# One q load per pair of heads, k copies split between ScalarE and the DMA queue, cluster rows stored in one transfer

## The chip, the core and the metric

The kernel runs on one core of a Trainium2 chip. A core has five engines with an instruction queue each: TensorE (PE, matmuls into PSUM), VectorE (DVE), ScalarE (ACT), GpSimd (POOL) and SyncE (SP), which here only issues transfers; 16 DMA engines move the data. The metric is device time in microseconds, from one execution of the whole program; the median of several runs is compared. On this kernel a difference of about 0.5% is what the measurement can tell from none.

## The reference

Queries, keys and values have shape (2, 8, 768, 64): two batches, eight heads, 768 positions, head size 64. Each head has 16 centroids. Every query and every key is assigned to the centroid of largest cosine; a query sees only the keys of its own cluster. Two MLPs follow, each 512 to 2048 to 512 on 1536 tokens.

```python
q_assign = np.argmax(np.einsum('bhsd,hcd->bhsc', q_n, c_n), axis=-1)
k_assign = np.argmax(np.einsum('bhsd,hcd->bhsc', k_n, c_n), axis=-1)
mask = q_assign[:, :, :, None] == k_assign[:, :, None, :]
scores = scale * np.matmul(q, k.transpose(0, 1, 3, 2))
scores = np.where(mask, scores, -1000000000.0)
attn = softmax(scores)                      # exp, row sum, division
x = np.matmul(attn, v)                      # to (1536, 512)
h = x @ w_in;  x = (h * np.clip(h + 3, 0, 6) / 6) @ w_out
h = x @ w_in2; out = softplus(h) @ w_out2
```

## The kernel before

**Blocks and stages.** The tokens form six blocks of 256 (batch b, block u of three). For each block and head the attention makes two chunks of 128 queries by 768 keys (`chunk`): score matmuls on TensorE, the row maximum on VectorE (line 944), the exponential on ScalarE (line 952), the reciprocal of the sum. For the later blocks the attention weights are split into two float16 parts (`split`, lines 463 and 471: ScalarE makes the high part, VectorE the low part) and turned by a transposing DMA from `hl` into `pt` (line 985); earlier ones are turned by TensorE matmuls (line 977). `attend` multiplies with v (line 1053). The first MLP of a finished block is laid between the attention of later blocks (lines 654 to 656, 1116, 1136); the weights are decoded by VectorE (lines 529 to 531, 601 to 603). The second MLP fills the time from about 470 us on.

**Cluster rows.** `assign` makes for each pair of heads a tile `oh` of 128 partitions by 384: row 64t + 32n + 16*odd + c is cluster c of the query (t = 0) or key (t = 1) of one head, for half n of the sequence. `store` writes it to a scratch tensor `ohd` in HBM (line 806), as two transfers of 64 partitions; the destination of each is viewed as (half n, row c, position s). The rows come back as the lower 16 rows of the operands of the score matmul, which so adds the mask: `rows0` (lines 866 to 875) for the first block, line 889 into `qa` and line 918 into `ka` for the others. For the first pair `rows0` reads `oh` itself, without the scratch tensor.

**q and k of the later blocks.** `pair` loads q of two heads into a tile `qd` of 128 partitions, twice: once in the lower and once in the upper 64 partitions (line 885), both heads beside each other. `prep`, two heads ahead of its use, makes from it `qa` (64 rows of rounded q, then the cluster rows) and `qb` (in one half of the partitions the rounded q, in the other the remainder): two ScalarE instructions (lines 919, 920) and one of VectorE (line 921). From k it builds once per batch and head `kb`, rounded k and remainder (lines 914, 915). `ka` holds a copy of the rounded k, moved there by a DMA from `kb` (line 917), and the cluster rows. `ka` has two buffers, so the next but one head waits for the score matmuls of the one two before; `qb` has three, the pair's `qa` two, `qd` one.

**What sets the order.** The program is written out in a plan of steps with due times in units of a block (the table `K`: `a0` and `a1` for `assign`, `i` and `o` for the weights, `m` for the MLP, and so on). Then `own_order` lists all instructions, and `list_schedule` places each with a price from `estimate` at the earliest time that its inputs, its engine and its buffers allow; the order that comes out on each engine's queue, SP's among them, is fixed in the program. A transfer is priced there by an issue of 580 ns, a rate per kind (`RATE`), a fixed latency and one queue that all transfers share; `slack` is added between an instruction and its users on another engine. The engines keep to that order whatever the real times are.

Of the kernel before, what the change touches and what calls it, by code (L numbers as in the profile page):

```python
# [8 lines left out]
F32 = mybir.dt.float32  # L9
F32R = mybir.dt.float32r  # L10
# [3 lines left out]
ACTF = mybir.ActivationFunctionType  # L14
# [7 lines left out]
W1E = ['dve', 'dve']  # L22

K = {
    'slack': (800, 250),
    'asx': 3,
    'qx': -1,
    'f1': [0],
# [1 line left out]
    'look': {'PE': 0, 'Activation': 0},  # L30
    'pcp': 1,
    'r0p': [1, 2, 3, 4],
    'a0': [-1.153, -0.043, 0.103, 0.303],
    'v0': 0.133,
    'v1': 3.116,
    'a1': [2.095, 2.095, 2.993, 3.179],
    'i': [0.472, 0.641, 0.98, 1.067],
    'il': [0.357, 0.4, 0.334, 0.212],
    'o': [1.18, 1.511, 1.585, 1.882],
    'ol': [0.179, 0.246, 0.223, 0.145],  # L40
    'wd': 0.089,
    'm': [1.41, 2.61, 3.59, 4.703, 6.29],
    'ml': [0.976, 0.75, 1.125, 0.983, 1.339],
    'gq': 3,
    'gr': 1,
    'ahead': 2,
    'lag0': 0.008,
    'lag': 0.226,
    'pl': {},
    'ohb': 2,  # L50
    'gv': 2,
    'gk': [3, 0],
    'gi': [-1, -1, -1],
    'lead': 0,
    'w2o': [1.36, 1.527],
    'ly': [1.133],
    'p4': [-0.643, 0.833],
    'p5': [0.797, 0.627],
    'o1': [1.323, 0.41],
    'w2': [0, -0.047, -0.049, 0.272],  # L60
    's2': [9, 15],
    'ly2': [0],
    'mo': [2, 0, 3, 1],
    'P': '',
    'qs': '',
    'x0': [2, 2, 2],
    'f0': [0, 1],
    'ze': [0],
    'w2e': [4.497],
    'w2l': 0.213,  # L70
    'tg': (),
    'we': [(1,), (0,), (0,), (0,)],
    'sb': (2, 2),
    'w2d': 0.223,
    't3': 3.93,
    'w2s': 'left',
    'te': [1, 0, 1, 0, 0, 0, 0, 0, 1, 0, 1, 0, 0, 0, 0, 0],
    'dgb': 2,
    'v2': -0.878,
    'dge': 0,  # L80
    'pg': 1,
    'pk': 1,
    'dsp': [0, 1],
    'ro': 0,
    'vp': [0.262, 0.043, -0.149, -0.211],
    'eqp': [1, 1, 1, 0],
    'qdb': 1,
    'kbe': [1, 1, 1, 1],
    'dl': 300,
    'pl_': 100,  # L90
    'w2oe': ['dve', 'dve'],
}
# [17 lines left out]
}  # L110
POOLS = sorted(set(OVER) | {p for l in OVER.values() for p in l}, key=len, reverse=True)
WINDOW = 3413.3
RATE = {"raw<in_moe_w_in": 271, "raw<in_moe_w_out": 302, "raw<in_moe2_w_in": 239, "raw<in_moe2_w_out": 345, "ka<kb": 173, "qd<in_q": 118, "rk<in_k": 220, "st<in_v": 224, "ydram<ys": 243, "yl<ydram": 164, "ka<ohd": 276, "q0<in_q": 203, "k0<in_k": 201, "rq<in_q": 232, "ohd<oh": 265, "qa<ohd": 165, "k0<ohd": 99, "q0<ohd": 109, "k0<oh": 39, "q0<oh": 39, "cw<in_centroids": 63}


def elements(a):
# [6 lines left out]
def estimate(op, eng, ins, outs, inst, psum):  # L123


    n = max([elements(a) for a in ins + outs] or [0])
# [5 lines left out]
    if eng == "PE":  # L132
        cols, f32 = elements(ins[0]), str(ins[0].dtype)
        m = inst.tile_size[1]
        if f32 == "dt.float32":
            t = max(cols * m / 76.8, 1.75 * m) + (90 if cols > 256 else 45 if cols > 128 else 5 if m == 128 else 40 if m == 64 else 27)
        else:
            t = cols / 2.4 + (15 if "32r" in f32 else 2.5)
# [28 lines left out]
        return t - 40, t + 60, op in ("TensorScalarPtr", "TensorTensor", "TensorCopy")  # L167
    size = max(elements(a) * list(a.ap)[0][1] * SIZE.get(str(a.dtype), 4) for a in ins + outs)
    if op == "DmaTransposeAnt":
        return 1640, (size / 250, K['dl'] - 500), False  # L170
    rate = RATE.get(outs[0].bass_ap.tensor.name.rsplit("_", 1)[0] + "<" + ins[0].bass_ap.tensor.name.rsplit("_", 1)[0], 200)
    return 580, (size / rate, K['dl']), False


class Graph:
# [90 lines left out]
def list_schedule(g, slack):  # L266
# [49 lines left out]
    for _ in range(N):  # L316
# [33 lines left out]
        queues[e].append(k)  # L350
        free[e] = s + hold
        if isinstance(done, tuple):
            time, lat = done
            queue = max(s + hold + 500, queue) + time
            done = queue + lat
        else:
            if shared:
                port[e] = s + done - (30 if e == "DVE" else 60)
            done += s
# [38 lines left out]
def kernel(ctx: ExitStack, tc: tile.TileContext, qT, kT, v, cen, w1i, w1o, w2i, w2o, out):  # L398
# [24 lines left out]
    one_s = const.tile([128, 128], F32)  # L423
    nc.vector.memset(one_s, 1.0)

    ohd = dram.tile([B, NP, 2, 2 * C, S], F32)
    ydram = dram.tile([NB, 128, KD, TB], F32)

    def after(tile_, src):
# [5 lines left out]
    def pace(tile_):  # L435

        if 0 in paced:
            if K["pcp"]:
                after(tile_, paced[0])
            else:  # L440
                nc.vector.tensor_copy(out=tile_[:, 0:1].bitcast(F32), in_=paced[0])
# [424 lines left out]
    def rows0(h):  # L866

        p, odd = divmod(h, 2)
        for t, dst in ((1, K0[h][64:64 + C]), (0, Q0[p][64:64 + C, odd])):
            if p == 0:  # L870
                for n in range(2):
                    r0 = 64 * t + 32 * n + C * odd
                    nc.sync.dma_start(out=dst[:, n * SH:(n + 1) * SH], in_=oh[0, p][r0:r0 + C, :])
            else:
                nc.sync.dma_start(out=dst, in_=ohd[0, p, t, C * odd:C * odd + C])

    def pair(b, u, p):

        qs = slice(u * TB, (u + 1) * TB)
        qd = rqp.tile([128, 2, TB], F32, tag="qd", name="qd", bufs=K["qdb"])  # L880
        if b == 0 and u == 1 and 2 * p < K["gq"]:
            pace(qd[:, 0])
        src = qT[b, 2 * p:2 * p + 2, :, qs].rearrange("o d s -> d o s")
        for half in range(2):
            nc.sync.dma_start(out=qd[64 * half:64 * half + 64], in_=src)
        qa = kq.tile([64 + C, 2, TB], F32R, tag="qa", name="qa", bufs=2)
        dst = qa[64:64 + C].bitcast(F32)
        src = ohd[b, p, 0, :, qs].rearrange("(o c) s -> c o s", o=2)
        nc.sync.dma_start(out=dst, in_=src)
# [750 lines left out]
```

## Time and profile before

| | before |
|---|---|
| median of 3 runs | 770.31 us (767.09 to 770.63) |
| the profiled execution's own time | 774.19 us |
| its span, first to last instruction | 772.2 us |
| TensorE busy | 718.1 us (93%) |
| VectorE busy | 608.8 us (79%) |
| ScalarE busy | 515.7 us (67%) |
| GpSimd busy | 96.0 us (12%) |
| mean granted TensorE clock | 0.976 of full |
| moved by DMA | 103.03 MB, mean 133 GB/s |

The profiled execution's time holds the span and some 2 us around it. Busy shares are averages over stages of different kinds: attention with the first MLP to about 470 us, the second MLP after that. TensorE's matmuls are pipelined, so a busy TensorE need not be at its peak. The DMA share of a stretch is the mean busy share of the 16 DMA engines; as it is put together from packets' times, it can lie above 1 in short stretches. "Idle before" and "waits" name what ended the idle time of an engine.

### The profile page before, as it was taken

Reading aid. Unit: us, or ns where it says so; the run is one execution under the profiler, and the core shown is the slowest. Engines: PE = TensorE matmul, PEld = TensorE weight load, DVE = VectorE, ACT = ScalarE, POOL = GpSimd, SP = SyncE. Lnnn points to the kernel's source line nnn. Section 1 sums busy time; section 2 is a strip of 40 time slices with the busy share of each in tenths; the row PEclk is TensorE's granted clock in tenths of the full one; section 3 lists DMA queues with packets and bytes.
Section 4 is the critical chain, followed back from the end, with each engine's and each line's share of the span. In section 5 each row is a group of like instructions: output and inputs, shape, how many; then the busy total and the mean of one; then the engine's idle time right before and its main releaser. Section 6 shows DMA issues by size and latency. Waiting matters only on the chain.

```text
span 772.2 us, 15821 instructions
## 1 busy us (share of the span) xinstructions
PE 718.1 (93%) x6173; PEld 601.6 (78%) x6173; DVE 608.8 (79%) x1101; ACT 515.7 (67%) x897; POOL 96.0 (12%) x170
## 2 busy tenths in 40 slices
PE   5679779999989988899999989999999999999998
PEld 1355566788778867788888878897888888888887
DVE  3457698999968767797899986998999998925930
ACT  1338668787778876796777775666786368726931
POOL 6021532331220220001000300000000000000000
PEclk9989989999999999999999999999999999999999
DMA  8174554788999996989999997141441020010001
GB/s 185 38 216 146 159 180 148 190 198 199 222 194 193 201 167 138 158 171 203 210 198 204 206 215 190 57 164 52 141 136 43 29 69 2 1 42 16 1 15 41
DMA packets 170906, 103.03 MB, mean 133 GB/s; under 512 B 130064, under 2 KB 155408, under 8 KB 170832
## 3 DMA queue, kind: packets, MB, share of 16 engines
q1 hardware_dynamic: 170832, 102.04, 57.4%
q8 instruction: 48, 0.79, 0.4%
q14 instruction: 26, 0.21, 0.1%
HBM read 57.77 MB, written 7.86 MB: 85 GB/s over the span
## 4 chain that ended last, share of the span: by engine, by line
PE 72%; DMA 10%; DVE 10%; ACT 3%; issue 2%; POOL 2%; SPq 0%; ACTq 0%; DVEq 0%; POOLq 0%
PE s L941 7%; DMA pt<-hl 5%; PE h L1353 5%; PE h L1354 5%; PE h L1355 5%; PE y L655 5%; PE y L654 5%; PE y L656 5%; PE avt L1053 5%; PE h L654 4%; PE h L656 4%; PE h L655 4%; PE o L1518 3%; PE o L1519 3%; PE o L1520 3%
## 5 line engine op out<-in xcount | busy, mean ns | idle before, releaser
L944 DVE TENSOR_REDUCE nm<-s 128x1 f32<-128x768 f32 x96 | 90.8, 949 | 27.9 <-PE s L941 27.6
L654 PE MATMUL y<-g,w 128*128 128x256 f16 x384 | 105.9, 276 | 5.6 <-ACT ys L1136 4.9
L952 ACT ACTIVATE e<-s,nm 128x768 f32<-128x768 f32 x96 | 85.8, 894 | 37.5 <-DVE nm L948 17.3
L655 PE MATMUL y<-g,w 128*128 128x256 f16 x384 | 105.8, 275 | 1.4 <-DVE g L471 1.4
L656 PE MATMUL y<-g,w 128*128 128x256 f16 x384 | 105.8, 275 | 1.1 <-DVE w L471 1.1
L654 PE MATMUL h<-x,w 128*128 128x256 f16 x384 | 105.6, 275 | 0.0
L656 PE MATMUL h<-x,w 128*128 128x256 f16 x384 | 105.6, 275 | 0.0
L655 PE MATMUL h<-x,w 128*128 128x256 f16 x384 | 105.4, 275 | 0.0
L1354 PE MATMUL h<-y,w 128*128 128x256 f16 x336 | 90.8, 273 | 0.0
L1353 PE MATMUL h<-y,w 128*128 128x256 f16 x336 | 90.3, 273 | 0.0
L1355 PE MATMUL h<-y,w 128*128 128x256 f16 x336 | 89.7, 273 | 0.0
L655 PEld LDWEIGHTS <-w 128*128 128x128 f16 x768 | 75.9, 99 | 17.2 <-issue 8.4
L654 PEld LDWEIGHTS <-w 128*128 128x128 f16 x768 | 76.4, 100 | 15.8 <-issue 6.3
L656 PEld LDWEIGHTS <-w 128*128 128x128 f16 x768 | 76.1, 99 | 15.1 <-issue 4.6
L463 ACT ACTIVATE hl<-e,r 128x768 f16<-128x768 f32 x72 | 66.7, 929 | 28.7 <-DMA pt<-hl 21.7
L471 DVE SCALAR_TENSOR_TENSOR hl<-e,r,hl 128x768 f16<-128x768 f32 x72 | 73.3, 1025 | 14.9 <-ACT hl L463 14.1
L471 DVE SCALAR_TENSOR_TENSOR g<-a,sg,g 128x512 f16<-128x512 f32 x72 | 51.5, 744 | 4.2 <-ACT g L463 3.9
L941 PE MATMUL s<-kb,qb 128*128 128x384 f32 x160 | 49.2, 386 | 4.2 <-ACT e L952 4.1
L1053 PE MATMUL avt<-pt,v 128*64 128x256 f16 x648 | 46.9, 287 | 6.3 <-DMA pt<-hl 6.3
L977 PEld LDWEIGHTS tr<-dg,e 128*128 128x128 f32 x288 | 39.4, 209 | 14.3 <-issue 8.4
L463 ACT ACTIVATE g<-a,sg 128x512 f16<-128x512 f32 x72 | 48.5, 712 | 1.3 <-DVE a L1413 0.7
L1053 PEld LDWEIGHTS <-v 128*64 128x64 f16 x648 | 37.5, 115 | 14.8 <-issue 8.3
(234 smaller groups left out, 1685.9 us busy)
## 6 DMA issues: line engine op xcount, KB each, us to landing
raw<-in_moe_w_out_dram SPq DMA_DIRECT2D x32, 512.0 KB
raw<-in_moe_w_in_dram SPq DMA_DIRECT2D x8, 1024.0 KB
raw<-in_moe_w_in_dram SPq DMA_DIRECT2D x16, 512.0 KB
ka<-kb SPq DMA_DIRECT2D x40, 192.0 KB
qd<-in_q_dram SPq DMA_DIRECT2D x40, 128.0 KB
rk<-in_k_dram SPq DMA_DIRECT2D x12, 384.0 KB
st<-in_v_dram SPq DMA_DIRECT2D x12, 256.0 KB
ydram<-ys SPq DMA_DIRECT2D x12, 256.0 KB
```

What stands on the lines that cost most here:

```text
L463: nc.scalar.activation(out=hi, in_=src, func=ACTF.Copy, scale=scale)
L471: nc.vector.scalar_tensor_tensor(out=lo, in0=src, scalar=scale, in1=hi, op0=ALU.mult, op1=ALU.subtract)
L654: nc.tensor.matmul(out=ps, lhsT=wt.lhsT(kk, m, 0), rhs=xh, start=start, stop=False)
L655: nc.tensor.matmul(out=ps, lhsT=wt.lhsT(kk, m, 0), rhs=xl, start=False, stop=False)
L656: nc.tensor.matmul(out=ps, lhsT=wt.lhsT(kk, m, 1), rhs=xh, start=False, stop=stop)
L941: nc.tensor.matmul(out=s[:, n, 0:SH], lhsT=x[:, q], rhs=y[:, n * SH:(n + 1) * SH], start=i == 0, stop=i == len(pairs) - 1)
L944: nc.vector.tensor_reduce(out=nm, in_=sv, op=ALU.max, axis=AX.XY, negate=True)
L952: nc.scalar.activation(out=e.rearrange("p (a s) -> p a s", a=2), in_=sv, func=ACTF.Exp, bias=nm, scale=scale, accum_out=sm)
L1053: nc.tensor.matmul(out=a[64 * odd:64 * odd + 64, p % 2, :], lhsT=vt[:, kt, vi, odd, :], rhs=PT[2 * p + odd][:, pi * KT + kt, :], start=(kt ...
L1353: nc.tensor.matmul(out=ps[:, o, :], lhsT=hi, rhs=y[:, 0, kk], start=first and o == kk == 0, stop=False, skip_group_check=True)
L1354: nc.tensor.matmul(out=ps[:, o, :], lhsT=hi, rhs=y[:, 1, kk], start=False, stop=False, skip_group_check=True)
L1355: nc.tensor.matmul(out=ps[:, o, :], lhsT=lo, rhs=y[:, 0, kk], start=False, stop=kk == 1, skip_group_check=True)
```

## The change

Three things are done in another way, and the order is laid out anew.

1. `qd` holds each pair's q once, head 2p in the lower and head 2p + 1 in the upper 64 partitions: one transfer in place of two. `qa` and `qb` become two slots of one pair's tile of 128 partitions. One ScalarE instruction writes the rounded q into the lower 64 rows of both slots (64x512 by a repeated input), another one writes the 64 rows that VectorE subtracts from (64x256).
2. `ka`'s copy of the rounded k is made by ScalarE for odd heads (`kac` 0) and by the DMA for even heads (`kac` 3).
3. `ohd` keeps the halves of the sequence apart, in the order of `oh`'s partitions, so that `store` is one transfer of 128 partitions by 384. The loads of cluster rows are viewed accordingly; q's rows of the middle block (positions 256 to 511) cross the halves at 384 and are fetched in two transfers.
4. The table `K` has other due times and slack, and `estimate` prices transfers by one rate with a lead time in place of a rate per kind.

```diff
-    'slack': (800, 250),
+    'slack': (150, 300),
-    'a0': [-1.153, -0.043, 0.103, 0.303],
+    'a0': [-0.937, -0.118, 0.131, 0.512],
-    'a1': [2.095, 2.095, 2.993, 3.179],
+    'a1': [2.223, 2.078, 2.909, 3.267],
...
-    'dl': 300,
+    'dl': 200,
+    'kac': [3, 0],
...
-RATE = {"raw<in_moe_w_in": 271, "raw<in_moe_w_out": 302, ...}
+RATE = 272
...
     if op == "DmaTransposeAnt":
-        return 1640, (size / 250, K['dl'] - 500), False
-    rate = RATE.get(...)
-    return 580, (size / rate, K['dl']), False
+        return 1640, (size / 157, 400 + K["dl"], 800), False
+    return 580, (size / RATE, 850 + K["dl"], 1080), False
...
-            time, lat = done
-            queue = max(s + hold + 500, queue) + time
+            time, lat, lead = done
+            queue = max(s + lead, queue) + time
...
-    ohd = dram.tile([B, NP, 2, 2 * C, S], F32)
+    ohd = dram.tile([B, NP, 2, 2, 2 * C, SH], F32)
...
     def store(b, p):
-        for t in range(2):
-            nc.sync.dma_start(out=ohd[b, p, t].rearrange("c (n s) -> n c s", n=2), in_=oh[b, p][64 * t:64 * t + 64])
+        nc.sync.dma_start(out=ohd[b, p].rearrange("t n c s -> (t n c) s"), in_=oh[b, p])
...
-                nc.sync.dma_start(out=dst, in_=ohd[0, p, t, C * odd:C * odd + C])
+                nc.sync.dma_start(out=dst.rearrange("c (n s) -> c n s", n=2), in_=ohd[0, p, t, :, C * odd:C * odd + C].rearrange("n c s -> c n s"))
...
-        qd = rqp.tile([128, 2, TB], F32, tag="qd", name="qd", bufs=K["qdb"])
+        qd = rqp.tile([128, TB], F32, tag="qd", name="qd", bufs=K["qdb"])
...
-        src = qT[b, 2 * p:2 * p + 2, :, qs].rearrange("o d s -> d o s")
-        for half in range(2):
-            nc.sync.dma_start(out=qd[64 * half:64 * half + 64], in_=src)
-        qa = kq.tile([64 + C, 2, TB], F32R, tag="qa", name="qa", bufs=2)
-        dst = qa[64:64 + C].bitcast(F32)
-        src = ohd[b, p, 0, :, qs].rearrange("(o c) s -> c o s", o=2)
-        nc.sync.dma_start(out=dst, in_=src)
+        nc.sync.dma_start(out=qd, in_=qT[b, 2 * p:2 * p + 2, :, qs].rearrange("h d s -> (h d) s"))
+        qa = kq.tile([128, 2, 2, TB], F32R, tag="qa", name="qa", bufs=2)
+        dst = qa[64:64 + C, :, 1].bitcast(F32)
+        s0, s1 = qs.start, qs.stop
+        while s0 < s1:
+            n, e = s0 // SH, min(s1, (s0 // SH + 1) * SH)
+            src = ohd[b, p, 0, n, :, s0 - n * SH:e - n * SH].rearrange("(o c) s -> c o s", o=2)
+            nc.sync.dma_start(out=dst[:, :, s0 - u * TB:e - u * TB], in_=src)
+            s0 = e
...
-        qb = kq.tile([128, TB], F32R, tag="qb", name="qb")
...
-        nc.sync.dma_start(out=ka[0:64].bitcast(F32), in_=kb[here].bitcast(F32))
-        nc.sync.dma_start(out=ka[64:64 + C].bitcast(F32), in_=ohd[b, p, 1, C * odd:C * odd + C])
-        nc.scalar.activation(out=qb, in_=qd, func=ACTF.Copy, scale=0.125)
-        nc.scalar.activation(out=qa[0:64], in_=qd[0:64], func=ACTF.Copy, scale=0.125)
+        e = K["kac"][h % len(K["kac"])]
+        if e == 0:
+            nc.scalar.activation(out=ka[0:64], in_=kb[here].bitcast(F32), func=ACTF.Copy)
...
+        else:
+            nc.sync.dma_start(out=ka[0:64].bitcast(F32), in_=kb[here].bitcast(F32))
+        nc.sync.dma_start(out=ka[64:64 + C].bitcast(F32).rearrange("c (n s) -> c n s", n=2), in_=ohd[b, p, 1, :, C * odd:C * odd + C].rearrange("n c s -> c n s"))
+        qa, qb = qq[0:64 + C, 1], qq[:, 0]
+        if odd:
+            nc.scalar.activation(out=qb[here], in_=qd[here], func=ACTF.Copy, scale=0.125)
+            nc.scalar.activation(out=qq[0:64], in_=qd[here].unsqueeze(1).broadcast_to([64, 2, TB]), func=ACTF.Copy, scale=0.125)
+        else:
+            nc.scalar.activation(out=qq[0:64], in_=qd[here].unsqueeze(1).broadcast_to([64, 2, TB]), func=ACTF.Copy, scale=0.125)
+            nc.scalar.activation(out=qb[there], in_=qd[here], func=ACTF.Copy, scale=0.125)
         nc.vector.scalar_tensor_tensor(out=qb[here], in0=qd[here], scalar=0.125, in1=qb[here].bitcast(F32), op0=ALU.mult, op1=ALU.subtract)
```

The other entries of `K` that change are due times of the same kind (for v, the weights and the MLP steps).

## Rows read from the trace of the kernel before

**Rows 1.** Windows: us, busy us of each engine, clock, DMA share, GB/s

```profile
140.00:225.00 85.00, 79.87 (x685) 67.21 (x684) 78.87 (x160) 68.39 (x124) 21.58 (x35) 0.96 0.85 198
225.00:345.00 120.00, 111.61 (x1025) 94.85 (x1022) 91.73 (x164) 94.27 (x176) 17.89 (x34) 0.97 0.95 175
345.00:470.00 125.00, 122.25 (x1136) 104.11 (x1134) 108.07 (x193) 92.00 (x164) 11.77 (x22) 0.99 1.04 205
```

**Rows 2.** Waits of PE, in stretches 0:45, 45:100, 140:225 and 225:345

```profile
PE s L941 <- DMA k<-ohd: 7.0, 1, 7.0
PE s L941 <- DMA k<-ohd: 2.4, 1, 2.4
PE s L941 <- DMA ka<-ohd: 2.1, 1, 2.1
PE avt L1053 <- DMA pt<-hl: 3.9, 2, 2.5
PE y L654 <- ACT ys L1136: 3.7, 1, 3.7
```

**Rows 3.** Chain that ended last, whole span: start us, us, what

```profile
32.20 6.22 DMA ohd<-oh
73.42 6.71 DMA ohd<-oh
208.94 7.01 DMA ka<-ohd
266.76 9.24 DMA pt<-hl
276.87 0.83 ACT ys L1136 x2
298.23 6.47 DMA pt<-hl
399.18 8.25 DMA pt<-hl
```

**Rows 4.** Timeline of SP's issues, around three stores

```profile
31.65 1.03 SPq L806 DMA_DIRECT2D ohd<-oh  x2
36.60 0.31 SPq L875 DMA_DIRECT2D q<-ohd  x1
207.68 1.22 SPq L806 DMA_DIRECT2D ohd<-oh  x2
265.52 1.14 SPq L806 DMA_DIRECT2D ohd<-oh  x2
```

**Rows 5.** Windows of 1 and 4 us behind the stores

```profile
34.00:35.00 1.00, 0.00 (x0) 0.00 (x0) 0.83 (x2) 0.08 (x2) 0.00 (x0) 1.00 0.13 37
295.00:296.00 1.00, 1.00 (x11) 0.62 (x8) 1.00 (x2) 0.61 (x3) 0.60 (x1) 1.00 0.12 13
216.00:220.00 4.00, 3.91 (x17) 2.96 (x18) 2.89 (x6) 2.79 (x7) 0.00 (x0) 0.57 0.98 96
```

**Rows 6.** DMA issues by line, whole span

```profile
ka<-kb SPq DMA_DIRECT2D x40, 192.0 KB
qd<-in_q_dram SPq DMA_DIRECT2D x40, 128.0 KB
ohd<-oh SPq DMA_DIRECT2D x16, 96.0 KB
```

**Rows 7.** Groups by line, shapes apart: busy us, mean ns, idle before

```profile
L919 ACT ACTIVATE qb<-qd 128x256 fp32r<-128x256 f32 x40 | 16.0, 407 | 5.7 <-PE s L941 3.9 <-DMA qd<-in_q_dram 1.7
L920 ACT ACTIVATE qa<-qd 64x256 fp32r<-64x256 f32 x40 | 15.0, 406 | 4.5 <-DMA qd<-in_q_dram 3.5 <-POOL dg L966 0.8 <-PE s L941 0.2
L914 ACT ACTIVATE kb<-rk 64x768 fp32r<-64x768 f32 x16 | 13.4, 839 | 0.8 <-DMA rk<-in_k_dram 0.6
```

**Rows 8.** Waits of SP's queue, whole span

```profile
SPq L917 <- PE s L941: 19.2, 9, 9.1
SPq L917 <- ACT kb L914: 10.1, 3, 6.2
```

More of the change, by code (lines that the diff above doesn't have):

```diff
@@ L32 @@
     'r0p': [1, 2, 3, 4],
-    'a0': [-1.153, -0.043, 0.103, 0.303],
-    'v0': 0.133,
-    'v1': 3.116,
-    'a1': [2.095, 2.095, 2.993, 3.179],
[L37 to L43, printed above, removed]
+    'a0': [-0.937, -0.118, 0.131, 0.512],
+    'v0': 0.158,
+    'v1': 3.02,
+    'a1': [2.223, 2.078, 2.909, 3.267],
+    'i': [0.471, 0.639, 0.98, 1.067],
+    'il': [0.354, 0.399, 0.323, 0.205],
+    'o': [1.182, 1.511, 1.585, 1.881],
+    'ol': [0.179, 0.317, 0.272, 0.153],
+    'wd': 0.09,
+    'm': [1.41, 2.61, 3.59, 4.703, 6.383],
+    'ml': [0.98, 0.767, 1.125, 0.983, 1.25],
     'gq': 3,
@@ L46 @@
     'ahead': 2,
-    'lag0': 0.008,
-    'lag': 0.226,
+    'lag0': 0.029,
+    'lag': 0.23,
     'pl': {},
@@ L54 @@
     'lead': 0,
[L55 to L62, printed above, removed]
+    'w2o': [1.318, 1.319],
+    'ly': [1.067],
+    'p4': [0.105, 0.385],
+    'p5': [0.754, 0.522],
+    'o1': [1.695, 1.358],
+    'w2': [0, 0.292, -0.148, 0.768],
+    's2': [5, 12],
+    'ly2': [6],
     'mo': [2, 0, 3, 1],
@@ L68 @@
     'ze': [0],
-    'w2e': [4.497],
-    'w2l': 0.213,
+    'w2e': [4.39],
+    'w2l': 0.285,
     'tg': (),
@@ L73 @@
     'sb': (2, 2),
-    'w2d': 0.223,
-    't3': 3.93,
+    'w2d': 0.215,
+    't3': 3.55,
     'w2s': 'left',
@@ L78 @@
     'dgb': 2,
-    'v2': -0.878,
+    'v2': -1.732,
     'dge': 0,
@@ L84 @@
     'ro': 0,
-    'vp': [0.262, 0.043, -0.149, -0.211],
+    'vp': [0.425, 0.339, 0.09, -0.22],
     'eqp': [1, 1, 1, 0],
@@ L112 @@
 WINDOW = 3413.3
-RATE = {"raw<in_moe_w_in": 271, "raw<in_moe_w_out": 302, "raw<in_moe2_w_in": 239, "raw<in_moe2_w_out": 345, "ka<kb": 173, "qd<in_q": 118, "rk<in_k": 220, "st<in_v": 224, "ydram<ys": 243, "yl<ydram": 164, "ka<ohd": 276, "q0<in_q": 203, "k0<in_k": 201, "rq<in_q": 232, "ohd<oh": 265, "qa<ohd": 165, "k0<ohd": 99, "q0<ohd": 109, "k0<oh": 39, "q0<oh": 39, "cw<in_centroids": 63}
+RATE = 272
 def elements(a):
@@ L169, in estimate @@
     if op == "DmaTransposeAnt":
-        return 1640, (size / 250, K['dl'] - 500), False
-    rate = RATE.get(outs[0].bass_ap.tensor.name.rsplit("_", 1)[0] + "<" + ins[0].bass_ap.tensor.name.rsplit("_", 1)[0], 200)
-    return 580, (size / rate, K['dl']), False
+        return 1640, (size / 157, 400 + K["dl"], 800), False
+    return 580, (size / RATE, 850 + K["dl"], 1080), False
 class Graph:
@@ L874, in rows0 @@
             else:
-                nc.sync.dma_start(out=dst, in_=ohd[0, p, t, C * odd:C * odd + C])
+                nc.sync.dma_start(out=dst.rearrange("c (n s) -> c n s", n=2), in_=ohd[0, p, t, :, C * odd:C * odd + C].rearrange("n c s -> c n s"))
     def pair(b, u, p):
         qs = slice(u * TB, (u + 1) * TB)
-        qd = rqp.tile([128, 2, TB], F32, tag="qd", name="qd", bufs=K["qdb"])
+        qd = rqp.tile([128, TB], F32, tag="qd", name="qd", bufs=K["qdb"])
         if b == 0 and u == 1 and 2 * p < K["gq"]:
-            pace(qd[:, 0])
-        src = qT[b, 2 * p:2 * p + 2, :, qs].rearrange("o d s -> d o s")
-        for half in range(2):
-            nc.sync.dma_start(out=qd[64 * half:64 * half + 64], in_=src)
-        qa = kq.tile([64 + C, 2, TB], F32R, tag="qa", name="qa", bufs=2)
-        dst = qa[64:64 + C].bitcast(F32)
-        src = ohd[b, p, 0, :, qs].rearrange("(o c) s -> c o s", o=2)
-        nc.sync.dma_start(out=dst, in_=src)
+            pace(qd)
+        nc.sync.dma_start(out=qd, in_=qT[b, 2 * p:2 * p + 2, :, qs].rearrange("h d s -> (h d) s"))
[7 more added lines that the diff above has]
+            s0 = e
         KP[p] = b, u, qd, qa
@@ L898, in prep @@
             pair(b, u, p)
-        of_, qd, qa = KP[p][:2], KP[p][2][:, odd], KP[p][3][:, odd]
+        of_, qd, qq = KP[p][:2], KP[p][2], KP[p][3][:, odd]
         if of_ != (b, u):
@@ L916, in prep @@
         kb = KB[h]
-        nc.sync.dma_start(out=ka[0:64].bitcast(F32), in_=kb[here].bitcast(F32))
-        nc.sync.dma_start(out=ka[64:64 + C].bitcast(F32), in_=ohd[b, p, 1, C * odd:C * odd + C])
-        nc.scalar.activation(out=qb, in_=qd, func=ACTF.Copy, scale=0.125)
-        nc.scalar.activation(out=qa[0:64], in_=qd[0:64], func=ACTF.Copy, scale=0.125)
+        e = K["kac"][h % len(K["kac"])]
+        if e == 0:
+            nc.scalar.activation(out=ka[0:64], in_=kb[here].bitcast(F32), func=ACTF.Copy)
+        elif e == 1:
+            nc.gpsimd.tensor_copy(out=ka[0:64], in_=kb[here].bitcast(F32))
+        elif e == 2:
+            nc.vector.tensor_copy(out=ka[0:64], in_=kb[here].bitcast(F32))
+        else:
[8 more added lines that the diff above has]
+            nc.scalar.activation(out=qb[there], in_=qd[here], func=ACTF.Copy, scale=0.125)
         nc.vector.scalar_tensor_tensor(out=qb[here], in0=qd[here], scalar=0.125, in1=qb[here].bitcast(F32), op0=ALU.mult, op1=ALU.subtract)
```

## The prediction

> **What bounds the kernel now.** I read the windows by stage first [rows 1]. From 140 to 470 us TensorE is busy for 313.7 of 330 us, VectorE for 278.7, ScalarE for 254.7, and the DMA share rises from 0.85 over 0.95 to 1.04. So TensorE sets the pace, the DMA engines are full beside it, and ScalarE has 75 us free. A faster time can come only from TensorE's idle time (5.1, 8.4 and 2.75 us in the three stretches), from the stalls ahead of 140 us, and from stretches in which the granted clock lay under 1.
>
> Second, the waits of TensorE [rows 2]: the long ones are for a transfer, 7.0 and 2.4 us for the k rows of the first block, 2.1 us for the cluster rows of ka, 3.9 us in two pieces for a transposed tile. The wait of 3.7 us put down to ScalarE's ys is a transfer too: in the chain the ys copy at 276.87 comes behind a transpose of 9.24 us that began at 266.76 [rows 3].
>
> Third, the rest of that chain, with the queue that issues the transfers beside it [rows 4]. The chain passes through a store of cluster rows for 6.22 and for 6.71 us. The 7.01 us at 208.94 begin where the two stores issued at 207.68 end; the 9.24 us begin behind the two issued at 265.52; the 6.47 us at 298.23 have another pair some 5 us ahead. Five long stalls have a pair of stores ahead of them. The 8.25 us at 399.18 have none, as the stores are over by then: a full queue alone can hold a transpose as long.
>
> **Why a store is slow.** While nothing but a store moved, from 34 to 35 us, the DMA share was 0.13 at 37 GB/s [rows 5]. That is two engines of 16 at some 18 GB/s each (37 / 2). From 295 to 296, with a store in flight and other work queued, it was 0.12 again: the rest of the queue gets little done. The destination's slowest dimension in line 806 is the half n, of size 2.
>
> **The stores, changed.** The new one writes 128 rows by one pattern. The kernel's other transfers, led by 16, 64 or 128 rows, bring the DMA share to 1.04 [rows 1], so such a pattern can use all 16 engines, and I take 16. One of 96 KB [rows 6] is 98,304 B, so 49,152 B for each of two engines, 2.7 us at 18 GB/s. The first of the pair at 31.65 had landed at 36.60 [rows 4], 4.4 us after its own half of the 1.03 us issue; 1.7 us of that is not data. The new store has 196,608 B, 12,288 B for each of 16 engines, 0.7 us: 2.4 us in all, against 6.22. The bounds are 6.22 (no help) and 2.4. The rows of q could be fetched after the first store of a pair, and now wait for the whole; at 2.4 us that is still ahead of the 4.4.
>
> What it frees, stall by stall: (a) 7.0 us: 3.8. (b) 2.4 us: all, the shorter store being 4.3 us less late. (c) 2.1, (d) 3.7 and (e) the longer piece of the 3.9, 2.5: all, if the transfers behind a store no longer queue for two engines. Sum 14.5 us. Behind such a stall TensorE's clock is also low: 0.57 granted from 216 to 220 [rows 5], that is 3.4 us at 1.2 GHz of its two levels 1.2 and 2.4, after the wait of 2.1 us; 4 x 0.43 = 1.7 us of full speed. For five stalls 8.5 us. The ceiling is 23 us and the floor is 0.
>
> I take half, 11.5 us. What is late next explains the half: VectorE is busy for 78.87 of 85 us in the stretch of (c), so matmuls brought forward there soon wait for its results; in (d) and (e) the transposes still share a full queue, as at 399.18.
>
> **q once, and ka.** 40 loads of 128 KB become 20 of 128 KB, and 20 of the 40 copies of 192 KB leave [rows 6]: 20 x 131,072 + 20 x 196,608 B = 6.6 MB. At the 198, 175 and 205 GB/s of the full stretches [rows 1] that would be 32 to 37 us of the DMA engines, but these means are those of transposes; it may be half. It lies beside TensorE's work, and so it is worth only what the waits for transposes still hold: at most the 1.4 us left of the 3.9 and the 2.75 us idle after 345 us. Between 0 and 4.2 us I take 1, as the idle of a queue that stays full.
>
> SP issues 20 q loads, 20 copies and 8 stores fewer; the cluster rows of q for the middle block are cut at 384, 8 issues more. At some 0.5 us each (half of 1.03 [rows 4]) the 40 issues are 20 us of SP over some 350 us, and the transposes stand in the same queue behind them. That lies behind TensorE's work and is counted in the 1 us; where TensorE waited for SP throughout, it would be worth the 20.
>
> **ScalarE's share.** The qb instruction of 128x256 (407 ns) and the qa of 64x256 (406 ns) [rows 7] give way to 64x512 and 64x256. Between 64x256 at 406 and 64x768 at 839, 64x512 comes to 622: +0.215 us for each of 40 heads, 8.6 us. The 20 copies of 64x768 into ka cost 0.839 each like the kb copy, 16.8 us. ScalarE has 25.4 us more, of 75 us free. ScalarE works in order: a copy into ka waits until the head two before has left the buffer, and behind it wait an exp (then VectorE's reciprocal, the split, a transpose) or a PSUM bank that TensorE wants back. SP waited 19.2 us for that release and 10.1 us for kb [rows 8], so half of these 29.3 us, 14.7, may move to ScalarE. The cost lies between 0 (25.4 + 14.7 = 40.1 us still fit in 75) and 40.1; near the lower end, as free time is twice that: 2.5 us, a tenth of the work. VectorE's, GpSimd's and TensorE's instructions stay the same in number and shape. qb had three buffers of one head each and now lies in the pair's tile, of which there are two: room for four heads, so no new wait there.
>
> **The order.** Due times, slack and the planner's transfer prices change, so work moves. By the text, a small transfer is planned from issue to use at 580 + 500 + 300 + 800 = 2,180 ns plus data before and 1,080 + 850 + 200 + 150 = 2,280 after, so no large shift follows from it; a transpose of 393,216 B goes from 4,313 to 4,055 ns but holds the planned queue 2.5 in place of 1.6 us. What moved due times are worth no row shows. The bound is the idle time in 140 to 470 that no store explains, 16.3 - 8.3 = 8 us, either way; I take 0.
>
> **Sum.** -11.5 - 1 + 2.5 + 0 = -10 us against the profiled execution, 774.19 us (span 772.2 and 2 around it): 764.2. The median of the runs, 770.31, is 3.9 lower, so 760.3; I say 761.
>
> **Rivals.** *The stores give nothing.* The Trainium skill (DMA: Bandwidth & Descriptors, Rules for kernel authors) says of two transfers to disjoint partition halves that both spray over all 16 engines, so that joining them gains little; by that rule a joined store would land about as late as the second of the pair did. The share of 0.13 speaks against it. As a mechanism of this kernel: the long landing is the write to HBM, or VectorE's results are what is really late in each place. Then -1 + 2.5, about 772 us.
>
> *ScalarE becomes the bound.* The place is the ka copy of the odd heads, between the exps, from 140 to 470. At 40.1 us moved and half of it on the path, 20 us against 12.5 of gains: 770.3 + 7.5, about 778. It decides from 12.5 of the 40 us on. For it: the exp, the split and the MLP's copies all stand behind such a copy in one queue. Against it: 75 us free.
>
> *All the stalls go.* 23 + 4.2 - 0 = 27 us: 743. For it: the five stalls share one cause. Against it: VectorE beside them.
>
> **How the numbers follow.** Forecast 0.50 (754 to 767, its own range), all stalls gone 0.15 (743 to 754), stores give nothing 0.17 (768 to 774), ScalarE 0.18 (774 to 785). Cutting about 0.1 at either end, I give 748 to 776. A change of 0.5% (3.9 us) is about what the measurement can tell; under 766.5 counts as faster, over 774.2 as slower: 0.65, 0.18 and 0.17.
>
> **What would show it.** Right: the store of cluster rows lands within 3 us of its issue; TensorE's wait for the first k rows falls from 7.0 to about 3; no stall of over 2 us follows a store after 200 us; ScalarE's busy time rises from 515.7 to about 541. Wrong: the same stalls in the same places with a store of full DMA share ahead, or ScalarE's waits for TensorE at the ka copy and TensorE's waits for exp grown by over 10 us; or new stalls where no touched instruction stands, which would be the order's.

## The result, and the profile after

The kernel after takes 750.16 us (median of 4 runs, 747.09 to 751.07) against 770.47 beside it: ratio 0.9728, 95% interval 0.9674 to 0.9782, so 20.3 us or 2.6% less. The direction was forecast and the time lies inside the range, but the gain is more than twice the 9.3 us forecast; it is nearest to the rival in which all the stalls go (743). The profiled execution took 749.29 us, its span is 747.5, and the mean granted clock rose from 0.976 to 0.991 of full.

The windows of the kernel after, in the stretches of [rows 1] (us, busy us of TensorE, its weight loads, VectorE, ScalarE, GpSimd, then clock, DMA share, GB/s):

```profile
140.00:225.00 85.00, 79.44 (x714) 66.32 (x712) 78.64 (x151) 75.67 (x129) 13.82 (x27) 0.98 0.89 204
225.00:345.00 120.00, 119.80 (x1120) 101.51 (x1118) 99.52 (x176) 108.55 (x190) 17.63 (x39) 0.99 0.82 159
345.00:470.00 125.00, 124.26 (x1170) 107.04 (x1170) 112.08 (x196) 97.39 (x160) 11.48 (x11) 1.00 0.83 173
```

TensorE's idle time from 225 to 345 fell from 8.4 to 0.2 us, and the DMA share there from 0.95 to 0.82. ScalarE is at 108.55 of 120 us. From 140 to 225 the idle time did not fall (5.1 to 5.6 us), though the work in a stretch is not the same in both kernels: more matmuls are done by 225 (714 against 685 in the stretch).

The waits of TensorE after, in the stretches 0:45, 45:100, 140:225 and 225:345, against [rows 2]:

```profile
PE s L954 <- DMA q<-oh: 2.1, 1, 2.1
PE s L954 <- DMA q<-ohd: 0.8, 1, 0.8
...
PE tr L990 <- ACT pt L994: 2.1, 3, 1.0
...
PE s L954 <- ACT e L965: 3.9, 3, 3.4
...
PE h L654 <- DVE r L1130: 0.2, 1, 0.2
```

None of the five old waits is left at its size. The 7.0 us for the first k rows are 0.8 us for q rows, and from 225 to 345 no transfer stands in the list. In these stretches what is left behind 45 us is ScalarE's and VectorE's, but for 0.3 us. The longest piece, 3.4 us at 177 us, ends with an exp that stands on ScalarE's queue behind four copies of weights:

```profile
176.20 2.55 ACT L463 ACTIVATE w<-st,wf 128x512 f16<-128x512 f32 x4
...
179.47 0.88 ACT L965 ACTIVATE e<-s,nm 128x768 f32<-128x768 f32 x1
...
180.50 0.74 PE L954 MATMUL s<-kb,qa 128*128 128x384 f32 x2 [3.36 <-ACT e L965]
```

The change touches neither the weight copies nor this exp. By the prediction's third sign of being wrong, a new stall where no touched instruction stands, it would be the order's; that ScalarE's added work has a part in it is not excluded.

The chain that ended last in the kernel after, whole span: of its longest pieces only one is a transfer, where [rows 3] show stores of 6.22 and 6.71 us and four more.

```profile
386.06 6.78 DMA pt<-hl
```

That no store is left among these pieces is what counts here. The transposes say less: the chain of s_wide, the experiment below that is as fast, still holds seven of them, of 3.9 to 9.1 us.

SP's issues after, around the first two stores (start us, us, what), against [rows 4]:

```profile
21.86 0.58 SPq L805 DMA_DIRECT2D ohd<-oh  x1
23.96 0.33 SPq L889 DMA_DIRECT2D qa<-ohd  x1
...
27.00 0.34 SPq L805 DMA_DIRECT2D ohd<-oh  x1
29.21 0.41 SPq L509 DMA_DIRECT2D raw<-in_moe_w_in_dram  x1
29.73 0.66 SPq L874 DMA_DIRECT2D k<-ohd  x1
```

The store issued at 27.00 had landed by 29.73 us, when its rows were fetched, 2.4 us after the end of its issue, as forecast. Over the eight stores the median from issue to landing is 2.1 us (the last number of this row of the DMA issues):

```profile
ohd<-oh SPq DMA_DIRECT2D x8, 192.0 KB, 2.1
```

ScalarE's prices came out as worked out from [rows 7]: 842 ns for a k copy (839 taken), 629 for 64x512 (622), 414 for 64x256 (406). These are the groups by line, of the q copies those of the odd heads:

```profile
L919 ACT ACTIVATE ka<-kb 64x768 fp32r<-64x768 f32 x20 | 16.8, 842 | 2.5 <-PE s L954 2.0
L930 ACT ACTIVATE qa<-qd 64x512 fp32r<-64x512 f32 x20 | 12.6, 629 | 0.4
L929 ACT ACTIVATE qa<-qd 64x256 fp32r<-64x256 f32 x20 | 8.3, 414 | 0.4
```

### The profile page after: what moved, and what is told of

It is laid out like the page before. It is cut to its first block, busy times and chain, and to the rows that moved or that the text cites. A ratio compares the mean times of both kernels' runs of the same rounds, so it can differ in the third digit from the quotient of the medians.

```text
span 747.5 us, 15758 instructions
## 1 busy us (share of the span) xinstructions
PE 706.8 (95%) x6173; PEld 593.7 (79%) x6173; DVE 612.5 (82%) x1101; ACT 545.1 (73%) x917; POOL 98.4 (13%) x170
## 4 chain that ended last, share of the span: by engine, by line
PE 57%; DVE 9%; ACT 5%; issue 2%; DMA 1%; POOL 0%; ACTq 0%; DVEq 0%; POOLq 0%
PE s L954 5%; PE avt L1066 4%; PE h L1366 4%; PE h L1368 4%; PE h L1367 4%; PE h L654 4%; PE y L654 4%; PE y L655 4%; PE h L656 4%; PE h L655 4%; PE y L656 3%; PE o L1533 3%; PE o L1532 3%; PE o L1531 3%; PE y L1495 2%
## 5 line engine op out<-in xcount | busy, mean ns | idle before, releaser
L655 PEld LDWEIGHTS <-w 128*128 128x128 f16 x768 | 76.4, 99 | 13.8 <-issue 5.0
L471 DVE SCALAR_TENSOR_TENSOR hl<-e,r,hl 128x768 f16<-128x768 f32 x72 | 75.3, 1052 | 7.8 <-ACT hl L463 7.3
L954 PE MATMUL s<-kb,qa 128*128 128x384 f32 x160 | 49.1, 382 | 6.6 <-ACT e L965 4.8
L990 PEld LDWEIGHTS tr<-dg,e 128*128 128x128 f32 x288 | 35.1, 191 | 16.0 <-issue 9.3
L990 PE MATMUL tr<-dg,e 128*128 128x128 f32 x288 | 39.1, 282 | 7.5 <-ACT pt L994 5.4
L1066 PE MATMUL avt<-pt,v 128*64 128x256 f16 x648 | 44.0, 275 | 0.0
```

Source lines behind the costliest of these rows:

```text
L471: nc.vector.scalar_tensor_tensor(out=lo, in0=src, scalar=scale, in1=hi, op0=ALU.mult, op1=ALU.subtract)
L655: nc.tensor.matmul(out=ps, lhsT=wt.lhsT(kk, m, 0), rhs=xl, start=False, stop=False)
L954: nc.tensor.matmul(out=s[:, n, 0:SH], lhsT=x[:, q], rhs=y[:, n * SH:(n + 1) * SH], start=i == 0, stop=i == len(pairs) - 1)
L990: nc.tensor.matmul(out=tr[:, kt, :], lhsT=e[:, (k0 + kt) * 128:(k0 + kt + 1) * 128], rhs=dg, start=True, stop=True)
```

## The experiments

Any edit that changes an instruction changes the planner's list, and the order on all queues is then laid anew. So the main experiments keep the order of one of the two kernels on every queue and change one thing under it; their traces have every engine's instructions and SP's issues in that kernel's order, one by one. In the diffs "..." stands for what is left out.

**All stores wide, order of the kernel before kept (s_wide).** The columns of the constant matrix that makes `oh` are interleaved, so that row 64t + 2(16 odd + c) + n holds what 64t + 32n + 16 odd + c held. The two stores of a pair stay two, of 64 rows each, in their places.

```diff
-        nc.vector.tensor_scalar(out=firstb[:, 0:64], in0=jb[:, 0:64], scalar1=-1.0, ...)
+        nc.vector.tensor_scalar(out=firstb[:, 0:64].rearrange("p (c n) -> p n c", n=2), in0=jb[:, 0:64].rearrange("p (n c) -> p n c", n=2), scalar1=-1.0, ...)
...
-            nc.sync.dma_start(out=ohd[b, p, t].rearrange("c (n s) -> n c s", n=2), in_=oh[b, p][64 * t:64 * t + 64])
+            nc.sync.dma_start(out=ohd[b, p, t].rearrange("c (n s) -> (c n) s", n=2), in_=oh[b, p][64 * t:64 * t + 64])
```

> The kernel before, its order on every queue kept, with one thing changed: the rows of oh stand in another order (a permuted constant matrix), so that each of the two stores of a pair is led by 64 rows and not by a dimension of 2. Theory A (the stores on two engines make the stalls): about 750 to 755 us, the k-row wait of 7.0 us falls to 3 or 4, and no stall of over 2 us behind a store. Theory B (the new order brings the gain): 765 to 771. Theory C (fewer q loads and copies relieve the queue and the DMA engines): 763 to 770, the waits for transposes stay.

748.55 us (746.29 to 749.38) against 771.43: ratio 0.9692 (0.9665 to 0.9718), 22.9 us less, 1.5 us under Theory A's range. That is as much as the kernel after gains, with q still loaded twice, all k copies on the DMA and not one instruction moved. So the gain needs neither Theory B nor Theory C. Whether they have a share in the kernel after is another question (s_narrow, below). A second run of the same kernel beside later ones took 747.35 (ratio 0.9718, 0.9671 to 0.9765).

SP's issues in this kernel show where the time is won:

```profile
24.90 1.23 SPq L806 DMA_DIRECT2D ohd<-oh  x2
27.15 0.34 SPq L889 DMA_DIRECT2D qa<-ohd  x1
27.78 0.32 SPq L918 DMA_DIRECT2D ka<-ohd  x1
28.20 1.09 SPq L806 DMA_DIRECT2D ohd<-oh  x2
30.40 0.31 SPq L875 DMA_DIRECT2D q<-ohd  x1
...
36.04 1.10 SPq L806 DMA_DIRECT2D ohd<-oh  x2
...
193.01 1.66 SPq L806 DMA_DIRECT2D ohd<-oh  x2
...
249.06 1.18 SPq L806 DMA_DIRECT2D ohd<-oh  x2
```

The second pair's store starts at 28.20 in place of 31.65 [rows 4], 3.5 us earlier though the first one started 0.5 us later. The fifth starts at 193.01 in place of 207.68, a lead of 14.7 us; the seventh pair's, at 249.06, answers to 265.52, 16.5 us. The span ends 26.2 us earlier (746.0); the profiled execution of before was 3.9 us over its median, so the medians show less, 22.9.

```profile
PE 707.3 (95%) x6173; PEld 593.9 (80%) x6173; DVE 609.7 (82%) x1101; ACT 515.1 (69%) x897; POOL 97.9 (13%) x170
```

Of the 26.2 us, 10.8 are TensorE's busy time (718.1 to 707.3, for the same 6173 matmuls, at a mean granted clock of 0.993 in place of 0.976) and 15.4 its idle time (54.1 to 38.7). The 7.0 us wait for the first k rows is gone; of all its waits for k rows this one is left:

```profile
PE s L941 <- DMA k<-ohd: 1.0, 1, 1.0
```

The first 4 us (3.5, and the 0.5 that the first store started late) are a wait that the prediction did not list. The waits of SP's queue in the kernel before, from 24 to 32 us:

```profile
SPq L889 <- DMA ohd<-oh: 3.6, 1, 3.6
SPq L918 <- DMA ohd<-oh: 1.5, 1, 1.5
```

SP's issues come in the program's order in the traces, and the loads of the first pair's rows (lines 889 and 918) stood ahead of the second pair's store. They waited 5.1 us for the first store's landing, and the second store behind them could not be issued. In s_wide they wait 1.2 us and are issued at 27.15 and 27.78. So the first k rows are fetched 7.5 us earlier (31.04 in place of 38.55): 3.5 as the second store starts earlier, 4.1 as it lands sooner.

**The store on two engines, order of the kernel after kept (s_narrow), and on four (s_narrow4).** A row of padding in the scratch tensor keeps the dimensions of the store apart; the number of transfers and their bytes stay.

```diff
-        nc.sync.dma_start(out=ohd[b, p].rearrange("t n c s -> (t n c) s"), in_=oh[b, p])
+        nc.sync.dma_start(out=ohd[b, p, :, 0:4 * C], in_=oh[b, p])        # s_narrow: led by 2
...
+        nc.sync.dma_start(out=ohd[b, p].rearrange("t n c s -> (t n) c s")[:, 0:2 * C], in_=oh[b, p])   # s_narrow4: led by 4
```

> The kernel after, its order kept, with one thing changed: the scratch tensor is padded by a row, so that the one store of a pair is led by a dimension of 2. Theory A: 765 to 772 us, the stalls behind the stores are back, each store landing 7 us or more after its issue. Theory B: 750 to 753. Theory C: 750 to 757.

> The kernel after in its own order, scratch rows padded so that the one store of a pair is led by a dimension of 4. Theory A (the number of engines counts): the data of a store take half as long as with 2 engines, so about half of the loss of 11.6 us: 754 to 758. Rival E (any pattern of more than two dimensions is slow, whatever leads it): 760 to 764.

With 2: 761.78 us (ratio to before 0.9872, 0.9847 to 0.9897), 11.6 over the kernel after, under Theory A's range and over those of B and C. With 4: 752.84 (0.9812, 0.9771 to 0.9853), 2.7 over it, less than expected; the intervals overlap, so it can't be told from none. So the count of engines decides, and not the number of dimensions (rival E falls). In this order the price of two engines is half of what it is in the order of before. The other half of the kernel after's gain is still there without the wide store: s_narrow is 9.7 us faster than before. So with slow stores the rest of the change wins something too, and what the store is worth depends on what stands around it. SP's issues in s_narrow, around the second store:

```profile
31.43 0.55 SPq L805 DMA_DIRECT2D ohd<-oh  x1
32.08 0.42 SPq L509 DMA_DIRECT2D raw<-in_moe_w_in_dram  x1
38.19 0.31 SPq L874 DMA_DIRECT2D k<-ohd  x1
```

The rows are fetched 6.2 us after the store's issue ended (38.19 - 31.98); in between the weights issued at 32.08 move too. The window of 1 us ahead of that shows what [rows 5] showed, a share of 2 engines in 16 with TensorE idle:

```profile
37.00:38.00 1.00, 0.00 (x0) 0.00 (x0) 0.00 (x0) 0.00 (x0) 0.00 (x0) 1.00 0.14 50
```

And in s_narrow4, where the same step takes 4.8 us (33.29 - 28.45), SP's issues and the window behind this store, with a share of 0.24, 4 engines in 16:

```profile
27.87 0.58 SPq L805 DMA_DIRECT2D ohd<-oh  x1
29.21 0.42 SPq L509 DMA_DIRECT2D raw<-in_moe_w_in_dram  x1
33.29 0.31 SPq L874 DMA_DIRECT2D k<-ohd  x1
```

```profile
29.00:30.00 1.00, 1.00 (x12) 1.00 (x11) 0.77 (x3) 0.25 (x1) 0.18 (x2) 1.00 0.24 26
```

SP's wait ahead of the second store shows here too: that store is issued at 27.00 us in the kernel after, at 27.87 with 4 engines and at 31.43 with 2 (the first store at 21.86, 21.91 and 23.60).

**Which stores (s_wide_b0, s_wide_b1).** As s_wide, with the scratch of one batch padded so that its stores stay on two engines.

```diff
-    ohd = dram.tile([B, NP, 2, 2 * C, S], F32)
+    ohd = [dram.tile([NP, 2, 2, C, S], F32, name="ohd"), dram.tile([NP, 2, 2, C + 1, S], F32, name="ohd")]   # s_wide_b0; the other way round in s_wide_b1
...
+            nc.sync.dma_start(out=ohd[b][p, t, :, 0:C].rearrange("o c (n s) -> o (c n) s", n=2), in_=oh[b, p][64 * t:64 * t + 64])
```

> The kernel before in its own order, rows of oh permuted; only the eight stores of the first batch (before 75 us) are led by 64 rows, those of the second batch by a dimension of 2. Theory A1 (each store costs where it stands): the lead over before is about 13 us at 150 us, as with all stores wide, and is kept: 756 to 760 us. Theory A2 (a lead won early is lost in waits of the full queue later): 762 to 768. Rival D (the row order, not the number of engines, brought the gain): 747 to 751, as the rows are permuted in both batches.

> The same with only the eight stores of the second batch (from 207 us on) led by 64 rows. Theory A1: no lead at 150 us, 9 to 12 us at the end: 758 to 763. Theory A2: 765 to 771. Rival D: 747 to 751.

The first batch alone: 755.77 against 768.52, 12.8 us less (ratio 0.9833, 0.9803 to 0.9864). The second alone: 757.91, 10.6 us less (0.9868, 0.983 to 0.9906). Both lie just under the ranges of A1. Together 23.4, and both at once gave 22.9: each batch's stores cost where they stand (A1), and the row order, which is the same in both, is not the cause (rival D falls).

**The instructions of one kernel in the planner of the other (a_all, b_none, b_wide).** Table `K` and the transfer prices are exchanged.

a_all is the code of the kernel after with the table, `RATE`, `estimate` and queue of before; b_none the code of the kernel before with those of after; b_wide is b_none with s_wide's edit, in b_none's order. From a_all:

```diff
-    'slack': (150, 300),
+    'slack': (800, 250),
...
-    'dl': 200,
+    'dl': 300,
...
-RATE = 272
+RATE = {"raw<in_moe_w_in": 271, "raw<in_moe_w_out": 302, ...}
```

> The instructions of the kernel after, ordered with the table and the transfer prices of the kernel before. Theory A: 748 to 758 us. Theory B: 764 to 772. Theory C: 750 to 758.

> The instructions of the kernel before, ordered with the table and the transfer prices of the kernel after. Theory A: 766 to 774 us, with long landings of the stores. Theory B: 750 to 757. Theory C: 763 to 772.

> The instructions of the kernel before, rows of oh permuted and all stores led by 64 rows, ordered with the table and the transfer prices of the kernel after. Against 785 with the same order prices and stores on two engines. Theory A: 765 or less; the distance to the kernel after, 750, is what q once and the k copies by ScalarE are worth in that order. If these are worth nothing: 748 to 755. If they matter because the table was made for them: 756 to 766.

a_all: 754.29 (0.9771, 0.9735 to 0.9806). b_none: 785.41 (1.0168, 1.014 to 1.0196), 14 us slower than the same instructions in the order of before. b_wide: 771.6 (1.0028, 1.0005 to 1.0051): the wide stores win 13.8 us there too (10.8 by the ratios to the runs of before beside each), but with q twice and the k copies on the DMA this planner's order is 21 us behind the kernel after (23 by the ratios). In the planner of before the same edits lose 5.7 us (754.29 against 748.55). Both comparisons include, beside q and the k copies, the joining of two wide stores into one, and the order is laid anew in each. So the edits cannot be given one worth; that an order serves the instructions that its table was made with would fit, but is not shown. Theory A had b_none at 766 to 774 and b_wide at 765 or less; both missed.

**What a new order alone is worth (w_dl320, b_dl180), and the two edits alone (w_q, w_kac).** In the first two no instruction changes, only the planner's latency entry: 300 to 320 ns under s_wide, 200 to 180 ns under the kernel after. The other two have wide stores and the table of before, one edit each.

```diff
-    'dl': 300,
+    'dl': 320,        # w_dl320
...
-    'dl': 200,
+    'dl': 180,        # b_dl180
```

> The instructions of the kernel with wide stores alone (748.6), all the same; only the planner's latency of a transfer goes from 300 to 320 ns, so that the order is laid anew. Theory G: 750 to 762, away from 748.6 by more than the measurement can tell. If the order is worth little: 746.5 to 750.5.

> The instructions of the kernel after, all the same; only the planner's latency entry goes from 200 to 180 ns, so that the order is laid anew. Theory G: 752 to 765. If the order is worth little: 748 to 752.

> Wide stores, q loaded once per pair, all copies of k by the DMA; table and transfer prices of the kernel before, so the order is laid anew. Against 748.6 with wide stores alone in before's own order and 754.3 with the k copies by ScalarE too. Theory C (the q load relieves queue and DMA engines): 744 to 748. Theory G (the order laid anew moves the time by several us whatever the edit): 749 to 760, with no stall at the q load in the trace.

> Wide stores, half of the k copies by ScalarE, q loaded twice; table and transfer prices of the kernel before, order laid anew. Theory H (ScalarE's 16.8 us more are partly on the path): 751 to 758, with TensorE's waits for the exp up by 3 us or more. Theory C: 744 to 748. Theory G: 749 to 760.

w_dl320: 754.1 (0.9778, 0.9725 to 0.9831), 5.5 us over s_wide; the interval is clear of s_wide's and overlaps that of its second run. b_dl180: 763.73 (0.9895, 0.9841 to 0.995), 13.6 us over the kernel after, clear of it. w_q: 753.48 (0.9771, 0.9707 to 0.9835), 4.9 us over s_wide; w_kac: 759.23 (0.9843, 0.9769 to 0.9917), 10.7 over. Both of the latter are within what a new order alone did (5.5 to 14 us in three cases), so theory G holds and neither says what the edit is worth. In w_kac TensorE's waits for the exp come to 8.9 us, 4.9 in s_wide, which points to theory H; with another order that is no proof. First s_wide, then w_kac:

```profile
PE s L941 <- ACT e L952: 4.9, 6, 1.7
```

```profile
PE s L945 <- ACT e L956: 8.9, 9, 2.5
```

**ScalarE's work and q's bytes, order kept (s_act, b_act, s_q15).** In s_act and b_act the 80 instructions for q also sum their rows into a tile that nobody reads; in s_q15 each q load takes 384 columns. The planner is shown the old sizes.

```diff
-        nc.scalar.activation(out=qb, in_=qd, func=ACTF.Copy, scale=0.125)
+        nc.scalar.activation(out=qb, in_=qd, func=ACTF.Copy, scale=0.125, accum_out=DM[...])   # s_act; the other q copies and b_act alike
...
-        qd = rqp.tile([128, 2, TB], ...)
+        qd = rqp.tile([128, 2, SH], ...)                                                      # s_q15
```

> The kernel of s_wide once more, as the base on this chip for the runs beside it: 747 to 750 us.

> The kernel of s_wide, its order on every queue kept; the 80 instructions of ScalarE that make qa and qb also sum their rows into a tile that nobody reads, which adds about 0.19 us each, 15 us of ScalarE, at their places. It stands for what the change lays on ScalarE there (25 us), without a new order. If ScalarE has the time free: within 1.5 us of s_wide2. Theory H (a tenth or more is on the path): 1.5 to 5 us over it. The rival of the prediction (half on the path): 7 us over it.

> The kernel of s_wide, its order kept; each of the 40 q loads moves 384 columns in place of 256, 2.6 MB more in all, as much as the change takes away by loading q once. Theory C (the bytes of q cost time): 1.5 to 6 us over s_wide2. If they lie beside other work: within 1.5 us of it.

> The kernel after, its order kept; the 80 instructions of ScalarE for q also sum their rows into a tile that nobody reads, about 15 us of ScalarE more. ScalarE is busy for 108.6 of 120 us from 225 to 345 there. If it has the time free: 749 to 752 us. Theory H: 752 to 756. Half on the path: 757 or more.

The dose came out smaller than meant. Here are the busy lines of s_wide2, s_act, the kernel after and b_act:

```profile
PE 707.8 (95%) x6173; PEld 595.3 (80%) x6173; DVE 610.0 (82%) x1101; ACT 515.1 (69%) x897; POOL 96.2 (13%) x170
```

```profile
PE 709.0 (95%) x6173; PEld 595.9 (80%) x6173; DVE 608.7 (81%) x1101; ACT 521.8 (70%) x977; POOL 97.3 (13%) x170
```

```profile
PE 706.8 (95%) x6173; PEld 593.7 (79%) x6173; DVE 612.5 (82%) x1101; ACT 545.1 (73%) x917; POOL 98.4 (13%) x170
```

```profile
PE 707.7 (94%) x6173; PEld 592.5 (79%) x6173; DVE 613.3 (82%) x1101; ACT 554.2 (74%) x997; POOL 94.6 (13%) x170
```

ScalarE's busy time rose by 6.7 us in s_act and by 9.1 in b_act, not by 15. The 80 reads of the sum are there, at 190 ns each in s_act, 15.2 us together, but they overlap their neighbours on the engine:

```profile
L919 ACT ACTIVATION_READ_ACCUMULATOR qb<-qd 128x1 f32 x40 | 7.6, 190 | 0.0
L920 ACT ACTIVATION_READ_ACCUMULATOR qa<-qd 64x1 f32 x40 | 7.6, 190 | 0.0
```

s_act took 748.29 (0.9722, 0.9681 to 0.9763), 0.9 over its base: nothing that can be told. b_act took 753.62 (0.9791, 0.9755 to 0.9827), 3.5 over the kernel after, which did not run beside it; the intervals overlap. s_q15 took 750.01 (0.9757, 0.9712 to 0.9801), 2.7 over its base, intervals overlapping as well. b_act and s_q15 lie in the ranges of theories H and C, s_act in that of free time; none of the three is clear of no effect.

## Why the prediction was wrong in size

**The step that failed** is the term of the stores: "I take half, 11.5 us". In the order of the kernel before, from whose rows the term was taken, and with nothing else changed, it is 22.9 us (s_wide), the ceiling that the prediction itself had worked out (23). Mechanism and place were right: 2 engines by the trace's 0.13, all the gain with a pattern led by 64 rows, a landing of 2.4 us.

Neither reason for the half shows in s_wide's trace. That "matmuls brought forward there soon wait for its results" was argued from VectorE's busy share in a stretch; that "the transposes still share a full queue", from one transpose. These are s_wide's windows, and TensorE's longest waits in the first and for transposes in the second:

```profile
140.00:225.00 85.00, 81.23 (x750) 69.54 (x747) 79.94 (x157) 70.18 (x127) 20.75 (x28) 1.00 1.00 217
225.00:345.00 120.00, 116.33 (x1086) 98.66 (x1084) 98.10 (x173) 96.87 (x182) 17.18 (x38) 0.99 0.98 180
```

```profile
PE y L654 <- ACT ys L1136: 2.7, 1, 2.7
PE y L656 <- DVE w L471: 1.1, 1, 1.1
...
PE avt L1053 <- DMA pt<-hl: 1.0, 2, 0.9
```

VectorE is as busy as before (79.94 against 78.87 us), and TensorE waits 1.1 us for one of its results there. The DMA engines are as full (0.98 against 0.95), and the waits for transposes fell from 3.9 to 1.0 us. TensorE's idle time from 140 to 345 fell from 13.5 to 7.4 us. The lead was not given back: 14.7 us at the fifth store, 16.5 at the seventh, 26.2 in the span at the end.

One wait was missing. The list of stalls began with TensorE's waits. A store that lands late also holds SP, and SP holds what stands behind it: 5.1 us ahead of the second pair's store, which stand in TensorE's waits only as part of the 7.0 us for the k rows. The prediction took 3.8 of these 7.0 as the most that could go, and all went.

That the ceiling was met is in part luck. Before the halving the prediction had 3.8 + 2.4 us and two stalls' clock for the first batch, 9.6 us, and 13.4 for the second; measured are 12.8 (s_wide_b0) and 10.6 (s_wide_b1). By kind, in the profiled executions, it had 14.5 us of idle time and 8.5 of the clock against 15.4 and 10.8. The landing of 2.4 us was worked out from 37 GB/s in one microsecond; in the two behind it the same share moved 45 and 49 GB/s.

**The terms do not add up one by one.** Read from the other end, the store is worth 11.6 us (the kernel after against s_narrow), what the prediction took, and then the rest of the change is worth 9.7 us (s_narrow against before), where the prediction had a loss of 1.5. With wide stores the rest is worth nothing that can be told: 750.16 against 748.55. Both ways are measured. So the wide stores alone are enough for the whole gain, and a new order with the other edits recovers part of what slow stores cost; by which edit, no run separates.

**q once and the ka copies, -1 us.** Not shown to be wrong, and not settled. 2.6 MB more of q cost 2.7 us in a fixed order, within the noise of two intervals; the prediction's ends for q and ka together were 0 and 4.2. The full queue that was its cover is less full after (0.82 from 225 to 345). With stores on two engines in the planner of after, the edits, with the joining of the two stores, are worth 24 us (b_none at 785.41, s_narrow at 761.78), the order laid anew.

**ScalarE, +2.5 us.** The prices were right, the sum a little low: 25.4 forecast, busy time up by 29.4 (545.1 - 515.7). What it costs is not settled: 0.9 us for 6.7 us of work in the order of before, 3.5 for 9.1 us in that of after, neither clear of the noise. The rival in which half of it is on the path would have had 3 to 5 us for these doses; b_act comes near that, s_act does not. The waits that the prediction let move to ScalarE, 14.7 us, came to 2.5 ahead of the ka copies (line 919); TensorE's waits for the exp went from 4.5 to 5.8 us and not up by the 10 that would have shown a stall there.

**The order, 0 with 8 us either way.** The bound was too small. The same instructions moved by 5.5, 13.6 and 14 us under another order, and the edits beside the wide stores cost 5.7 us or win 21 depending on the planner. "What moved due times are worth no row shows" was right, and the bound taken from idle time was no bound. The kernel after against s_wide is the sum of all that is not the wide store, where the stores are wide: it can't be told from 0.

**The rival from the rule** on two transfers to disjoint partition halves (the Trainium skill, DMA: Bandwidth & Descriptors, Rules for kernel authors) would have left the time at 772. That both halves use all 16 engines did not hold here: by the share of 0.13 the halves stood on two. Once each half is led by 64 rows the rule fits: two such stores (s_wide, 748.55) are as good as one of 128 (750.16), as far as runs tell that differ in their order too. That joining them gains little is the prediction's own conclusion from the rule; the row itself advises one transfer of 128 partitions, which fits as well.

**Versions.** The kernel with wide stores in the old order (748.55 and 747.35) and the kernel after (750.16) are the best; the measurement does not separate them, and no combination that was run beats them.

**Open.** What q once and the k copies by ScalarE are worth in one and the same order was not measured directly: removing or moving an instruction lays the order anew. Nor was the store's worth taken apart into the landing that TensorE waits for, the queue behind it and SP's wait.

## What to carry to other kernels

Read the leading dimension of every transfer's pattern, the destination's too, and check it in a stretch where it runs alone: a DMA share of 0.13 is 2 engines of 16. When a transfer lands late, list what the issuing queue holds behind it as well as who waits for its data; here that wait was missing from the list. Where a planner lays all queues, first measure what a new order alone does (here 5 to 14 us) and test an edit in a frozen order, or its worth is lost in that.

## What the runs showed of the hardware

Four engines in place of 16 cost 2.7 us in all (not clear of none), two cost 11.6, in the same order: the loss is far from proportional to the length of the transfer, with the step behind the second store at 4.8 us in the one and 6.2 us in the other. That the shorter one mostly hides behind other work is argued from this, not shown by a run of its own.

VectorE's instruction that makes the remainder of q kept its shape, 64x256, but took 497 ns in place of 423, 3 us in all, which the prediction did not count. The groups by line, first of the kernel before, then of the kernel after:

```profile
L921 DVE SCALAR_TENSOR_TENSOR qb<-qd,qb 64x256 fp32r<-64x256 f32 x40 | 16.9, 423 | 1.1 <-ACT qb L919 0.5
```

```profile
L934 DVE SCALAR_TENSOR_TENSOR qa<-qd,qa 64x256 fp32r<-64x256 f32 x40 | 19.9, 497 | 2.5 <-ACT qa L932 1.5 <-ACT qa L929 0.4
```

With the same instructions as the kernel after it took 497 ns in its order, 469 in that of b_dl180 and 468 in that of a_all; with those of before 423, and 440 in b_none. So the order has part in it. What in the order does it, and whether the form of the operands has part too, is open: b_act, in the order of the kernel after, has 454.

A summing copy on ScalarE comes with a read of the accumulator, 190 ns each in s_act, as the exp does (195 ns, line 952 of the kernel before). It overlaps the instructions ahead of it and behind it, so the engine's busy time rose by only 0.08 us each (6.7 / 80).
